# A three-layer kernel on one core: lower parts of weights made early and stored, and made by VectorE

## The chip, the cores and the metric

The kernel runs on one core of a Trainium2 chip. The metric is the device time of one execution in microseconds (us), as the median of several runs. TensorE (PE in the profile) does the matrix products, VectorE (DVE) and ScalarE (ACT) the elementwise work, GpSimd (POOL) a few more elementwise operations, and SyncE (SP) issues nearly all DMA transfers.

## The reference

```python
# attention without softmax: 8 batches, 8 heads, 576 positions, 64 wide
kv  = einsum('bhsd,bhse->bhde', k, v)
out = einsum('bhsd,bhde->bhse', q, kv)
x   = out / sqrt(mean(out*out, -1) + 1e-6) * g_norm     # then 4608 tokens x 512
# first MLP
h = x @ w_in                      # 512 -> 2048
x = maximum(0.01*h, h) @ w_out    # 2048 -> 512
# second MLP, own weights
h = maximum(x @ w_in2, 0)         # 512 -> 2048
y = (h*h) @ w_out2                # 2048 -> 512, the result
```

## The kernel before

The 4608 tokens are nine blocks of 512. The program runs four **passes** one after the other, each of them one large product: pass 1 is attention and the first product (`gemm1`, L560; 144 slots, 16 for a block), pass 2 the second (`second` with ph 0, L751), pass 3 the third (`first`, L687), pass 4 the fourth (`second` with ph 1, L751 again). In the profiled execution they begin at about 0, 513, 877 and 1228 us; the last products of pass 3 stand between the first ones of pass 4. What goes from one pass to the next goes through DRAM (`g`, `x2`).

TensorE multiplies in a rounded float32 format. To keep float32 accuracy each operand is held as an upper part ("hi", the rounded value) and a lower part ("lo", what rounding left), and each product is three matmuls: hi by hi, hi by lo, lo by hi. An upper part is a copy by ScalarE, the lower part a subtraction: source minus upper part. Passes 2 to 4 also use Strassen-Winograd's scheme: seven products of sums of quarters (S1..S4 of the left, T1..T4 of the right operand) instead of eight.

**Activations.** In pass 2 a step `gg` is one quarter of one block: seven products of 12 matmuls (128x256). For each step VectorE forms the sums T1 to T4 (`sum_op`, L631, tiles `sT`), ScalarE the seven upper parts (`hi_op`, L646, tiles `op_`) and VectorE the seven lower parts (`lo_op`, L651). After each block VectorE joins the seven results in seven additions (L666, `u` and `o_C`), the first of which takes a copy that ScalarE makes of a product (`p`, L762). In pass 3 the sums are joined into `h_C` (L666) and squared (L718).

**Weights.** Three of the four matrices are needed as Strassen operands: (0, 1) in pass 2, (1, 0) in pass 3 and (1, 1) in pass 4. Pass 1 prepares them beside its own work: `scale_w` and `join_w` scale the raw weights, `sum_w2` (L269, DVE 128x256, tiles `ws`) forms the sums, `store_w2` puts each 128x256 operand, unsplit, into DRAM as one half of a 256 KB slot (`w2_d`). Each matrix has 28 slots (NSLOT) of two halves. Before a slot is used, `fetch` loads it unsplit (L327), and `split_next` splits it some ticks later in the tile it lies in: ScalarE the upper (L314), GpSimd the lower part (L315, 128x2x256). That happens 84 times, 28 for each matrix: for pass 2 late in pass 1, for pass 3 half late in pass 2 and half in pass 3, for pass 4 in the last third of pass 3 and at the beginning of pass 4. GpSimd also makes the 28 lower parts of the squares that attention's norm sums (L475, in `stage_b`); TensorE uses them in `stage_t`.

**Order.** No scheduler moves anything: the program is one list, and each engine runs its instructions in the order in which that list issues them. Steps are put at slots of pass 1 (`put`) or at times counted in products (`at_slot`); pass 2 has 252 products, 7 for a step. A `store` is queued and issued on SP two ticks after its step. Larger tiles share 44 buffers (`take_big`), given out first in, first out; how many hold weights is bounded by `cap`.

Of the kernel before, what the change touches and what calls it, by code (L numbers as in the profile page):

```python
# [10 lines left out]
F32 = mybir.dt.float32  # L11
F32R = mybir.dt.float32r
U32 = mybir.dt.uint32
AF = mybir.ActivationFunctionType
ALU = mybir.AluOpType
# [3 lines left out]
def tile_linear_attention_two_mlps(  # L19
# [26 lines left out]
    nc = tc.nc  # L46
# [7 lines left out]
    P = 128  # L54
# [8 lines left out]
    TB = 512  # L63
# [25 lines left out]
    NSLOT = NPAIR * NPR // 2  # L89
# [14 lines left out]
    dram = ctx.enter_context(tc.tile_pool(name="dram", bufs=1, space=bass.MemoryType.DRAM))  # L104

    f32 = lambda t: t.bitcast(F32)
# [13 lines left out]
    w2_d = {  # L120
        x: [dram.tile([P, 2, U], F32, name=f"w2_{x[0]}{x[1]}_{n}") for n in range(NSLOT)]
        for x in ((0, 1), (1, 0), (1, 1))
    }
    g_d = [
        [[dram.tile([P, 2, 2, TB], F32, name=f"g{ph}_{j}_{n}") for n in range(NQ)] for j in range(NB)]
# [6 lines left out]
    def take_big(shape, dtype, name):  # L132
        n = big_free.pop(0)
        return big.tile(shape, dtype, tag=f"s{n}", name=name), n

    def give_big(*ns):
        big_free.extend(ns)
# [9 lines left out]
    w_t = {}  # L147
# [26 lines left out]
    w_pair = {}  # L174
# [53 lines left out]
    w_s = {}  # L228
    LEFT = {(0, 1): 0, (1, 0): 0, (1, 1): 1}

    def w_quarter(w, n, name):
        i, j = int(name[1]) - 1, int(name[2]) - 1
        if w[1] == 0:
            t = w_f[1, 2 * n + j, 0].rearrange("p (c f) -> p c f", c=2)
            return t[:, :, i * P:(i + 1) * P]
        k, o = (j, i) if LEFT[w] == 0 else (i, j)
        t = w_f[w[0], 2 * n + k, 1].rearrange("p (c f) -> p c f", c=4)
        return t[:, 2 * o:2 * o + 2, :]
# [7 lines left out]
    def store(out, in_, *slots):  # L246
        stores.append([out, in_, slots, 0])
# [16 lines left out]
    def sum_w2(w, n, name):  # L264
# [4 lines left out]
        nc.vector.tensor_tensor(out=t, in0=w_operand(w, n, a), in1=w_operand(w, n, b), op=op)  # L269
        w_s[w, n, name] = t  # L270

    def store_w2(w, n, name, last):
        x = [PRODUCTS[p][LEFT[w]] for p in ORDER].index(name)
        slot, half = divmod(NPR * n + x, 2)
        done = (w_s.pop((w, n))[1], w_pair.pop((*w, n))[1]) if last else ()
        store(
            w2_d[w][slot][:, half].rearrange("p (c f) -> p c f", c=2),
            w_s[w, n, name] if name[0] in "ST" else w_quarter(w, n, name), *done
        )
# [20 lines left out]
    w_split = []  # L300
# [5 lines left out]
    def w_halves(t):  # L306
        return f32(t).rearrange("p b (h e) -> p b h e", h=2)

    def split_next():
        w, slot, _ = w_split.pop(0)  # L310
        t = w_t[w, slot][0]
        by_h = t.rearrange("p b (h e) -> p b h e", h=2)
        src = w_halves(t)
        nc.scalar.activation(out=by_h[:, :, 0], in_=src[:, :, 1], func=AF.Copy)  # L314
        nc.gpsimd.tensor_tensor(  # L315
            out=by_h[:, :, 1], in0=src[:, :, 1], in1=src[:, :, 0], op=ALU.subtract
        )

    def fetch():
        while wanted and w_used[0] < w_cap[0] and big_free:  # L320
            if slot_n[0] < w_next[0]:
                break
            w_next[0] = slot_n[0] + w_pace[0]
            w, slot = wanted.pop(0)
            t, n = take_big([P, 2, TB], F32R, f"w2_{w[0]}{w[1]}_{slot}")
            w_used[0] += 1
            nc.sync.dma_start(out=w_halves(t)[:, :, 1], in_=w2_d[w][slot])  # L327
            w_t[w, slot] = t, n
            w_split.append([w, slot, 0])

    def drop_w(*keys):
        for key in keys:
# [20 lines left out]
    def at_tile(w, name):  # L353

        at_n[0] += 1
        return psum(at_n[0] % 8 if spare else 4 + at_n[0] % 4, name)[:, :w]
# [91 lines left out]
    def stage_b(i, p):  # L448
        qt, slot = qT.pop((i, p))
        hi, lo = qt[:, 0], qt[:, 1]  # L450
        ps = at_tile(TB, f"ops{i}_{p}")
        o = 0
        while o < TB:
            b, s = divmod(i * TB + o, S)
            n = min(TB - o, S - s)
            t = kv_t[(b * NP + p) % KV_BUFS]
            c = slice(o, o + n)
            if i == 0:
                nc.tensor.matmul(out=ps[:, c], lhsT=kvf_t[p], rhs=hi[:, c], start=True, stop=True)
                o += n  # L460
                continue
            nc.tensor.matmul(out=ps[:, c], lhsT=t[:, 0, :], rhs=hi[:, c], start=True, stop=False)
            nc.tensor.matmul(out=ps[:, c], lhsT=t[:, 0, :], rhs=lo[:, c], start=False, stop=False)
            nc.tensor.matmul(out=ps[:, c], lhsT=t[:, 1, :], rhs=hi[:, c], start=False, stop=True)
            o += n
        give_big(slot)
        sqo, slot = take_big([P, 2, TB], F32, f"sqo{i}_{p}")
        nc.scalar.activation(out=sqo[:, 0], in_=ps, func=AF.Square)
        nc.scalar.activation(out=sqo[:, 1], in_=ps, func=AF.Copy)
        if i < PLAIN_SS:  # L470
            sq_t[i, p] = (sqo, slot, None, None)
            return
        sqs, slot2 = take_big([P, 2, TB], F32R, f"sqs{i}_{p}")
        nc.vector.tensor_copy(out=sqs[:, 0], in_=sqo[:, 0])  # L474
        nc.gpsimd.tensor_tensor(  # L475
            out=sqs[:, 1], in0=sqo[:, 0], in1=f32(sqs[:, 0]), op=ALU.subtract
        )
        sq_t[i, p] = (sqo, slot, sqs, slot2)
# [321 lines left out]
    with tc.manual_schedule():  # L800
# [4 lines left out]
        for at0 in (3, 5, 6):  # L805
            w = jobs.pop(0)
# [6 lines left out]
        slots = [(j, m) for j in range(NB) for m in range(NM)]  # L813
# [33 lines left out]
        for s, (j, m) in enumerate(slots):  # L847
            if m == 0 and j + 1 < NB:
                at0, pace = (s - 5, 4) if j else (s, 4)
# [13 lines left out]
        def at_slot(t, *st):  # L863
            ev.append((t, st))
# [29 lines left out]
        t1 = 0  # L894
        t2 = second_pass(t1, 0, list(range(NB)))

        last = len(SETS) - 1
        insts = [(0, z) for z in range(last + 1)] + [(1, last), (1, 0)] + [
            (1, z) for z in range(last - 1, 0, -1)
# [4 lines left out]
        for x, (half, z) in enumerate(insts):  # L904
# [4 lines left out]
            again = x + 1 < len(insts) and insts[x + 1][1] == z  # L909
            if not (x and insts[x - 1][1] == z):  # L910
# [4 lines left out]
                for y, (kind, name) in enumerate(todo):  # L915
                    at0 = t0 - lead + 0.7 * y
                    if kind in ("oh", "ol"):
                        nth = [PRODUCTS[p][1] for p in ORDER].index(name)
                        if nth >= EARLY:
                            at0 = max(at0, t0 - 6.6 + 2 * (nth - EARLY) + (0.8 if kind == "ol" else 0))  # L920
                    elif name == "T4":
                        at0 = t0 - lead + 0.7 * y
                        at0 = max(at0, t0 - 6.6 + 2 * (4 - EARLY) + 0.9)
# [10 lines left out]
            for y, mine in enumerate(pairs):  # L934
                free = y == len(pairs) - 1 and not again
                for n in range(NPR):
                    at0 = t2 + NPR * u + 2 * n
                    at_slot(at0, "f", u, z, mine, n, free)
                    c = {2: "C11", 5: "C22", 4: "C21", 3: "C12"}.get(ORDER[n])
# [44 lines left out]
        def drop_pairs(ps):  # L984
# [9 lines left out]
            "const": constants, "gn": scale_g, "x": x_tiles, "kv": do_kv,  # L994
            "a": stage_a, "b": stage_b, "s": stage_s, "t": stage_t, "kvs": split_kv, "lo": relieve, "c": stage_c, "d": stage_d, "mlp": spare.clear,
            "scale": scale_w, "join": join_w, "w": split_w, "g1": gemm1, "lk": leaky,
            "ws": sum_w2, "w2": store_w2, "lag": set_lag, "want": want, "cap": cap, "xl": load_x, "gl": load_g2,
            "rawd": drop_raw, "os": sum_op, "sd": drop_sum, "oh": hi_op, "ol": lo_op,
            "tick": tick, "pace": set_pace, "f": first, "sq": square, "s2": second, "wd": drop_group, "wd3": drop_pairs,
        }  # L1000
# [30 lines left out]
        for kind, *args in prog:  # L1031
            do[kind](*args)
            if kind in free_by:
                n = load[free_by[kind]][1]
# [34 lines left out]
```

## Time and profile before

| | us |
|---|---|
| median of three runs | 1613.82 (1612.56 to 1617.27) |
| the profiled execution | 1613.53 |
| its span, first to last instruction | 1611.7 |
| PE busy | 1573.8 (98%) |
| DVE busy | 1207.9 (75%) |
| ACT busy | 792.6 (49%) |
| POOL busy | 165.9 (10%) |
| DMA, share of 16 engines by packets of the main queue | 57.4% |

An engine's share is an average over four passes with different limits, so the views below take stretches. "Busy" of PE counts a matmul at either clock: PEclk, the granted clock, tells which.

### The profile page before, as it was taken

Reading aid. Unit: us, or ns where it says so; the run is one execution under the profiler, and the core shown is the slowest. Engines: PE = TensorE matmul, PEld = TensorE weight load, DVE = VectorE, ACT = ScalarE, POOL = GpSimd, SP = SyncE. Lnnn points to the kernel's source line nnn. Section 1 sums busy time; section 2 is a strip of 40 time slices with the busy share of each in tenths; the row PEclk is TensorE's granted clock in tenths of the full one; section 3 lists DMA queues with packets and bytes.
Section 4 is the critical chain, followed back from the end, with each engine's and each line's share of the span. In section 5 each row is a group of like instructions: output and inputs, shape, how many; then the busy total and the mean of one; then the engine's idle time right before and its main releaser. Section 6 shows DMA issues by size and latency. Waiting matters only on the chain. (4 is left out here: it accounts for less than half of the span.)

```text
span 1611.7 us, 27476 instructions
## 1 busy us (share of the span) xinstructions
PE 1573.8 (98%) x10500; PEld 1425.2 (88%) x10500; DVE 1207.9 (75%) x1822; ACT 792.6 (49%) x1389; POOL 165.9 (10%) x124
## 2 busy tenths in 40 slices
PE   5999999999999999999999999999998999999999
PEld 3788888888888999999999888888887999999998
DVE  5766667676754888777778887668788988777776
ACT  5865565556555344444445454545455444444443
POOL 0001011111106200000004000310004400000000
PEclk8999999999999999999999999999999999999999
DMA  9968898989669244444346345555448344344442
GB/s 229 261 185 271 262 285 247 288 243 327 215 208 297 87 150 150 133 131 134 130 128 206 137 163 170 183 178 181 164 145 265 133 146 135 130 132 132 130 131 82
DMA packets 262755, 294.37 MB, mean 183 GB/s; under 512 B 54752, under 2 KB 225760, under 8 KB 262624
## 3 DMA queue, kind: packets, MB, share of 16 engines
q1 hardware_dynamic: 261024, 291.74, 57.4%
q8 instruction: 82, 1.34, 0.3%
q10 hardware_dynamic: 1600, 0.89, 0.2%
q14 instruction: 49, 0.40, 0.1%
HBM read 176.16 MB, written 116.39 MB: 182 GB/s over the span
## 5 line engine op out<-in xcount | busy, mean ns | idle before, releaser
L560 PE MATMUL hps<-xh,w 128*128 128x512 f32 x1152 | 380.4, 398 | 9.9 <-ACT w L220 5.7
L560 PEld LDWEIGHTS hps<-xh,w 128*128 128x128 f32 x1152 | 217.0, 189 | 59.1 <-ACT w L220 6.5
L560 PE MATMUL hps<-xl,w 128*128 128x512 f32 x576 | 225.5, 391 | 0.0
L315 POOL TENSOR_TENSOR w<-w 128x512 fp32r<-128x512 f32 x84 | 122.8, 1481 | 712.9 <-ACT w L314 394.3
L560 PEld LDWEIGHTS hps<-xl,w 128*128 128x128 f32 x576 | 108.9, 189 | 22.1 <-issue 1.0
L572 ACT ACTIVATE h<-hps 128x512 f32<-128x512 f32 x144 | 84.5, 596 | 47.5 <-DMA g<-h 21.1
L475 POOL TENSOR_TENSOR sqs<-sqo,sqs 128x512 fp32r<-128x512 f32 x28 | 41.1, 1467 | 395.7 <-DVE sqs L474 361.1
L503 DVE SCALAR_TENSOR_TENSOR sqo<-ssps,sqo 128x512 f32<-128x512 f32 x36 | 24.9, 692 | 72.2 <-ACT sqo L502 72.2
L666 DVE TENSOR_TENSOR h_C<-aps,u 128x512 f32<-128x512 f32 x72 | 49.5, 688 | 37.4 <-PE aps L687 37.3
L666 DVE TENSOR_TENSOR u<-bps,p 128x512 f32<-128x512 f32 x72 | 49.5, 688 | 32.0 <-ACT p L697 19.0
L718 DVE SCALAR_TENSOR_TENSOR h_C<-h_C 128x512 f32<-128x512 f32 x72 | 56.2, 781 | 0.0
L687 PE MATMUL aps<-op_B21h,w 128*128 128x512 f32 (+1 forms) x160 | 53.2, 381 | 2.4 <-ACT p L697 2.4
L687 PE MATMUL bps<-op_T4h,w 128*128 128x512 f32 (+1 forms) x160 | 51.8, 372 | 3.1 <-DVE u L666 3.1
L188 DVE SCALAR_TENSOR_TENSOR w_raw<-w_raw 128x512 uint32<-128x512 uint32 x64 | 48.6, 759 | 7.5 <-ACT w_raw L187 7.4
L687 PE MATMUL aps<-op_B22h,w 128*128 128x512 f32 (+1 forms) x160 | 52.0, 374 | 0.0
L697 ACT ACTIVATE p<-aps 128x512 f32<-128x512 f32 x36 | 21.2, 590 | 61.9 <-PE aps L687 61.9
L687 PE MATMUL bps<-op_T3h,w 128*128 128x512 f32 (+1 forms) x160 | 51.0, 368 | 0.0
L687 PE MATMUL bps<-op_T2h,w 128*128 128x512 f32 (+1 forms) x160 | 51.0, 368 | 0.0
L687 PE MATMUL aps<-op_T1h,w 128*128 128x512 f32 (+1 forms) x160 | 51.0, 368 | 0.0
L687 PE MATMUL aps<-op_B11h,w 128*128 128x512 f32 (+1 forms) x160 | 51.0, 368 | 0.0
L704 ACT ACTIVATE h_C<-aps 128x512 f32<-128x512 f32 x36 | 21.5, 598 | 58.9 <-issue 41.1
L314 ACT ACTIVATE w<-w 128x512 fp32r<-128x512 f32 x84 | 49.5, 618 | 0.0
(1405 smaller groups left out, 4041.7 us busy)
## 6 DMA issues: line engine op xcount, KB each, us to landing
g_raw<-g SPq DMA_DIRECT2D x144, 512.0 KB, 5.1
g<-h SPq DMA_DIRECT2D x144, 256.0 KB, 4.0
g<-h_C SPq DMA_DIRECT2D x144, 256.0 KB, 2.4
w<-w SPq DMA_DIRECT2D x84, 256.0 KB, 3.9
w_raw<-in_moe_w_in_dram SPq DMA_DIRECT2D x32, 512.0 KB, 6.5
w_raw<-in_moe_w_out_dram SPq DMA_DIRECT2D x32, 512.0 KB, 6.4
x_raw<-x SPq DMA_DIRECT2D x32, 512.0 KB, 5.9
w<-ws SPq DMA_DIRECT2D x96, 128.0 KB, 3.4
```

What stands on the lines that cost most here:

```text
L188: nc.vector.scalar_tensor_tensor(out=lower, in0=upper, scalar=0x80000000, in1=lower, op0=ALU.bitwise_and, op1=ALU.bitwise_or,)
L314: nc.scalar.activation(out=by_h[:, :, 0], in_=src[:, :, 1], func=AF.Copy)
L315: nc.gpsimd.tensor_tensor(out=by_h[:, :, 1], in0=src[:, :, 1], in1=src[:, :, 0], op=ALU.subtract)
L475: nc.gpsimd.tensor_tensor(out=sqs[:, 1], in0=sqo[:, 0], in1=f32(sqs[:, 0]), op=ALU.subtract)
L503: nc.vector.scalar_tensor_tensor(out=z, in0=ps, scalar=EPS, in1=z, op0=ALU.add, op1=ALU.mult)
L560: nc.tensor.matmul(out=ps, lhsT=w[:, wh, c * P:(c + 1) * P], rhs=x_t[j][xh, c // 2][0][:, c % 2, :], start=(c == 0 and y == 0), stop=(c == ...
L572: nc.scalar.activation(out=h, in_=h_ps.pop((j, m)), func=AF.Prelu, alpha=0.01)
L666: nc.vector.tensor_tensor(out=t, in0=x, in1=y, op=ALU.add)
L687: nc.tensor.matmul(out=ps[:, p], lhsT=w[:, wh, c, :], rhs=t[xh][:, c, :], start=(fresh and p == 0 and c == 0 and y == 0), stop=(p == len(p ...
L697: nc.scalar.activation(out=p1, in_=ps, func=AF.Copy)
L704: nc.scalar.activation(out=h, in_=ps, func=AF.Relu)
L718: nc.vector.scalar_tensor_tensor(out=h, in0=h, scalar=0.0, in1=h, op0=ALU.max, op1=ALU.mult)
```

## The change

Three things change.

1. **(1, 0), used in pass 3.** `store_w2` splits each of the 56 operand halves in pass 1, right where it stored them before: a ScalarE copy and a VectorE subtraction of 128x256 into a staging tile (`wh`, two halves in one buffer), then a store of 256 KB instead of 128 KB into a new DRAM array `w3_d`.
2. **(1, 1), used in pass 4.** It is stored unsplit in pass 1 as before. In pass 2 two new steps take each of its 28 slots: "rl" loads the slot (256 KB, tile `wr`), "rs" splits it five products later (ScalarE and VectorE, 128x2x256 each) and stores the 512 KB into `w3_d`. They stand evenly, one for every 6.86 products, from product 6 to 60 products before the end of pass 2.
3. **VectorE for GpSimd.** `split_loaded`, which now serves only (0, 1) and "rs", and the squares in `stage_b` take the lower part by VectorE. GpSimd is left with the constants at the start.

Passes 3 and 4 then load 512 KB for a slot instead of 256 KB and split nothing. In all, VectorE gains 28 + 28 + 28 subtractions of 128x512 elements and 56 of 128x256; GpSimd loses 112; ScalarE has 28 of 128x512 fewer and 56 of 128x256 more. The order of TensorE's matmuls is the same.

```diff
--- before.py
+++ after.py
@@ -121,6 +121,10 @@
         x: [dram.tile([P, 2, U], F32, name=f"w2_{x[0]}{x[1]}_{n}") for n in range(NSLOT)]
         for x in ((0, 1), (1, 0), (1, 1))
     }
+    w3_d = {
+        x: [dram.tile([P, 2, TB], F32, name=f"w3_{x[0]}{x[1]}_{n}") for n in range(NSLOT)]
+        for x in ((1, 0), (1, 1))
+    }
     g_d = [
         [[dram.tile([P, 2, 2, TB], F32, name=f"g{ph}_{j}_{n}") for n in range(NQ)] for j in range(NB)]
         for ph in range(2)
@@ -269,9 +273,23 @@
         nc.vector.tensor_tensor(out=t, in0=w_operand(w, n, a), in1=w_operand(w, n, b), op=op)
         w_s[w, n, name] = t
 
+    w_staged = []
+
     def store_w2(w, n, name, last):
         x = [PRODUCTS[p][LEFT[w]] for p in ORDER].index(name)
         slot, half = divmod(NPR * n + x, 2)
+        if w == (1, 0):
+            src = w_s[w, n, name] if name[0] in "ST" else w_quarter(w, n, name)
+            if not w_staged:
+                t, s = take_big([P, 2, 2, 2, P], F32R, f"wh{name}_{w[0]}{w[1]}_{n}")
+                w_staged.extend([(t[:, 0], ()), (t[:, 1], (s,))])
+            t, slots = w_staged.pop(0)
+            nc.scalar.activation(out=t[:, 0], in_=src, func=AF.Copy)
+            nc.vector.tensor_tensor(out=t[:, 1], in0=src, in1=f32(t[:, 0]), op=ALU.subtract)
+            store(w3_d[w][slot][:, half], f32(t).rearrange("p h c f -> p (h c f)"), *slots)
+            if last:
+                give_big(w_s.pop((w, n))[1], w_pair.pop((*w, n))[1])
+            return
         done = (w_s.pop((w, n))[1], w_pair.pop((*w, n))[1]) if last else ()
         store(
             w2_d[w][slot][:, half].rearrange("p (c f) -> p c f", c=2),
@@ -306,15 +324,31 @@
     def w_halves(t):
         return f32(t).rearrange("p b (h e) -> p b h e", h=2)
 
-    def split_next():
-        w, slot, _ = w_split.pop(0)
-        t = w_t[w, slot][0]
+    def load_unsplit(t, w, slot):
+        nc.sync.dma_start(out=w_halves(t)[:, :, 1], in_=w2_d[w][slot])
+
+    def split_loaded(t):
         by_h = t.rearrange("p b (h e) -> p b h e", h=2)
         src = w_halves(t)
         nc.scalar.activation(out=by_h[:, :, 0], in_=src[:, :, 1], func=AF.Copy)
-        nc.gpsimd.tensor_tensor(
+        nc.vector.tensor_tensor(
             out=by_h[:, :, 1], in0=src[:, :, 1], in1=src[:, :, 0], op=ALU.subtract
         )
+
+    def split_next():
+        w, slot, _ = w_split.pop(0)
+        split_loaded(w_t[w, slot][0])
+
+    w_again = {}
+
+    def load_again(w, slot):
+        w_again[w, slot] = t, n = take_big([P, 2, TB], F32R, f"wr_{w[0]}{w[1]}_{slot}")
+        load_unsplit(t, w, slot)
+
+    def split_again(w, slot):
+        t, n = w_again.pop((w, slot))
+        split_loaded(t)
+        store(w3_d[w][slot], f32(t), n)
 
     def fetch():
         while wanted and w_used[0] < w_cap[0] and big_free:
@@ -324,9 +358,12 @@
             w, slot = wanted.pop(0)
             t, n = take_big([P, 2, TB], F32R, f"w2_{w[0]}{w[1]}_{slot}")
             w_used[0] += 1
-            nc.sync.dma_start(out=w_halves(t)[:, :, 1], in_=w2_d[w][slot])
             w_t[w, slot] = t, n
-            w_split.append([w, slot, 0])
+            if w in w3_d:
+                nc.sync.dma_start(out=f32(t), in_=w3_d[w][slot])
+            else:
+                load_unsplit(t, w, slot)
+                w_split.append([w, slot, 0])
 
     def drop_w(*keys):
         for key in keys:
@@ -472,7 +509,7 @@
             return
         sqs, slot2 = take_big([P, 2, TB], F32R, f"sqs{i}_{p}")
         nc.vector.tensor_copy(out=sqs[:, 0], in_=sqo[:, 0])
-        nc.gpsimd.tensor_tensor(
+        nc.vector.tensor_tensor(
             out=sqs[:, 1], in0=sqo[:, 0], in1=f32(sqs[:, 0]), op=ALU.subtract
         )
         sq_t[i, p] = (sqo, slot, sqs, slot2)
@@ -893,6 +930,12 @@
 
         t1 = 0
         t2 = second_pass(t1, 0, list(range(NB)))
+
+        again = [(w, slot) for w in ((1, 1),) for slot in range(NSLOT)]
+        for x, key in enumerate(again):
+            at0 = t1 + 6 + (t2 - 60 - t1) * x / len(again)
+            at_slot(at0 + 0.05, "rl", *key)
+            at_slot(at0 + 5.05, "rs", *key)
 
         last = len(SETS) - 1
         insts = [(0, z) for z in range(last + 1)] + [(1, last), (1, 0)] + [
@@ -994,7 +1037,7 @@
             "const": constants, "gn": scale_g, "x": x_tiles, "kv": do_kv,
             "a": stage_a, "b": stage_b, "s": stage_s, "t": stage_t, "kvs": split_kv, "lo": relieve, "c": stage_c, "d": stage_d, "mlp": spare.clear,
             "scale": scale_w, "join": join_w, "w": split_w, "g1": gemm1, "lk": leaky,
-            "ws": sum_w2, "w2": store_w2, "lag": set_lag, "want": want, "cap": cap, "xl": load_x, "gl": load_g2,
+            "ws": sum_w2, "w2": store_w2, "lag": set_lag, "rl": load_again, "rs": split_again, "want": want, "cap": cap, "xl": load_x, "gl": load_g2,
             "rawd": drop_raw, "os": sum_op, "sd": drop_sum, "oh": hi_op, "ol": lo_op,
             "tick": tick, "pace": set_pace, "f": first, "sq": square, "s2": second, "wd": drop_group, "wd3": drop_pairs,
         }
```

VectorE in pass 2, step (1, 1), before: sums `sT` and lower parts `op0` of the right operand, one after the other.

```order
L651 TENSOR_TENSOR op0_(1, 1)_T2_5946<-sT2_0_(1, 1)_5940,op0_(1, 1)_T2_5946 128x512
L651 TENSOR_TENSOR op0_(1, 1)_B11_5962<-g_raw0_1_1_0_5807,op0_(1, 1)_B11_5962 128x512
L631 TENSOR_TENSOR sT3_0_(1, 1)_5982<-g_raw0_1_1_1_5809,g_raw0_1_1_0_5807 128x512
L651 TENSOR_TENSOR op0_(1, 1)_B21_5979<-g_raw0_1_1_1_5809,op0_(1, 1)_B21_5979 128x512
L651 TENSOR_TENSOR op0_(1, 1)_T3_5998<-sT3_0_(1, 1)_5982,op0_(1, 1)_T3_5998 128x512
L651 TENSOR_TENSOR op0_(1, 1)_T1_6013<-sT1_0_(1, 1)_5938,op0_(1, 1)_T1_6013 128x512
L631 TENSOR_TENSOR sT4_0_(1, 1)_6030<-g_raw0_1_1_1_5809,sT2_0_(1, 1)_5940 128x512
```

After, from the same row on, the split of one weight slot (`wr`) is among them.

```order
L688 TENSOR_TENSOR op0_(1, 1)_T2_6159<-sT2_0_(1, 1)_6153,op0_(1, 1)_T2_6159 128x512
L688 TENSOR_TENSOR op0_(1, 1)_B11_6175<-g_raw0_1_1_0_6015,op0_(1, 1)_B11_6175 128x512
L668 TENSOR_TENSOR sT3_0_(1, 1)_6195<-g_raw0_1_1_1_6017,g_raw0_1_1_0_6015 128x512
L688 TENSOR_TENSOR op0_(1, 1)_B21_6192<-g_raw0_1_1_1_6017,op0_(1, 1)_B21_6192 128x512
L688 TENSOR_TENSOR op0_(1, 1)_T3_6211<-sT3_0_(1, 1)_6195,op0_(1, 1)_T3_6211 128x512
L334 TENSOR_TENSOR wr_11_3_6133<-wr_11_3_6133 128x2x256
L688 TENSOR_TENSOR op0_(1, 1)_T1_6226<-sT1_0_(1, 1)_6151,op0_(1, 1)_T1_6226 128x512
L668 TENSOR_TENSOR sT4_0_(1, 1)_6245<-g_raw0_1_1_1_6017,sT2_0_(1, 1)_6153 128x512
```

`wr_11_3` stands between the lower parts of T3 and T1; the other 27 stand in the same way, each 0.14 product earlier in its step than the one ahead of it, once beside the lower parts and once beside the sums or additions.

ScalarE at that place, before: the upper parts of the same step.

```order
L646 ACTIVATE op0_(1, 1)_B21_5979<-g_raw0_1_1_1_5809 128x512
L646 ACTIVATE op0_(1, 1)_T3_5998<-sT3_0_(1, 1)_5982 128x512
L646 ACTIVATE op0_(1, 1)_T1_6013<-sT1_0_(1, 1)_5938 128x512
L646 ACTIVATE op0_(1, 1)_T4_6032<-sT4_0_(1, 1)_6030 128x512
L646 ACTIVATE op0_(1, 1)_B22_6047<-g_raw0_1_1_1_5809 128x512
```

After:

```order
L683 ACTIVATE op0_(1, 1)_B21_6192<-g_raw0_1_1_1_6017 128x512
L683 ACTIVATE op0_(1, 1)_T3_6211<-sT3_0_(1, 1)_6195 128x512
L683 ACTIVATE op0_(1, 1)_T1_6226<-sT1_0_(1, 1)_6151 128x512
L333 ACTIVATE wr_11_3_6133<-wr_11_3_6133 128x2x256
L683 ACTIVATE op0_(1, 1)_T4_6247<-sT4_0_(1, 1)_6245 128x512
L683 ACTIVATE op0_(1, 1)_B22_6263<-g_raw0_1_1_1_6017 128x512
```

The upper part of `wr_11_3` is behind that of T1, while VectorE takes the lower part of `wr_11_3` ahead of T1's.

VectorE in pass 1, fourth pair of (1, 0), before: sums of weights `ws`, the cast of squares `sqs`, the lower part of x (`xl`).

```order
L269 TENSOR_TENSOR ws_10_3_3250<-wp10_3_3182 128x256
L269 TENSOR_TENSOR ws_10_3_3250<-ws_10_3_3250,wp10_3_3182 128x256
L474 CAST sqs5_3_3279<-sqo5_3_3276 128x512
L518 TENSOR_TENSOR xl5_1_2959<-sqo5_2_3154,xh5_1_2958 128x512
L269 TENSOR_TENSOR ws_10_3_3250<-wp10_3_3182,ws_10_3_3250 128x256
L269 TENSOR_TENSOR ws_10_3_3250<-wp10_3_3182 128x256
```

After, from the same row on, with lower parts of weights `wh` (L288) and of squares (L512):

```order
L273 TENSOR_TENSOR ws_10_3_3359<-wp10_3_3291 128x256
L273 TENSOR_TENSOR ws_10_3_3359<-ws_10_3_3359,wp10_3_3291 128x256
L288 TENSOR_TENSOR whA22_10_2_3268<-ws_10_3_3359,whA22_10_2_3268 128x256
L288 TENSOR_TENSOR whA11_10_3_3364<-wp10_3_3291,whA11_10_3_3364 128x256
L511 CAST sqs5_3_3393<-sqo5_3_3390 128x512
L512 TENSOR_TENSOR sqs5_3_3393<-sqo5_3_3390,sqs5_3_3393 128x512
L555 TENSOR_TENSOR xl5_1_3043<-sqo5_2_3255,xh5_1_3042 128x512
L288 TENSOR_TENSOR whA11_10_3_3364<-ws_10_3_3359,whA11_10_3_3364 128x256
L288 TENSOR_TENSOR whA12_10_3_3400<-wp10_3_3291,whA12_10_3_3400 128x256
L273 TENSOR_TENSOR ws_10_3_3359<-wp10_3_3291,ws_10_3_3359 128x256
L273 TENSOR_TENSOR ws_10_3_3359<-wp10_3_3291 128x256
L288 TENSOR_TENSOR whA12_10_3_3400<-ws_10_3_3359,whA12_10_3_3400 128x256
```

Five `wh` and one `sqs` came between, two more `wh` follow; a `wh` that reads `ws` takes a sum that VectorE made one to three rows above and that ScalarE copies in between.

## Rows read from the trace of the kernel before

**Rows 1.** Page, busy time of each engine over the span and instructions.

```profile
PE 1573.8 (98%) x10500; PEld 1425.2 (88%) x10500; DVE 1207.9 (75%) x1822; ACT 792.6 (49%) x1389; POOL 165.9 (10%) x124
```

**Rows 2.** Waits of PE: line and releaser: us in total, times, longest.

```profile
PE ps L751 <- DVE h_C L666: 5.4, 1, 5.4
PE bps L687 <- DVE u L666: 3.1, 2, 2.8
...
PE ps L751 <- DVE u L666: 1.5, 1, 1.5
...
PE ps L751 <- POOL w L315: 1.0, 1, 1.0
```

**Rows 3.** Timeline, pass 3 to 4: start, us, engine, line, what, [idle before <-releaser].

```profile
1218.82 1.78 DVE L631 TENSOR_TENSOR sS_(7, 0)_12915<-g_raw,g_raw 128x512 f32<-128x512 f32 x1
1220.64 0.69 DVE L631 TENSOR_TENSOR sS_(7, 0)_12917<-sS_(7, 0)_12915,g_raw 128x512 f32<-128x512 f32 x1
...
1236.97 2.94 POOL L315 TENSOR_TENSOR w<-w 128x512 fp32r<-128x512 f32 x2 [5.00 <-DMA w<-w]
...
1238.72 1.75 DVE L631 TENSOR_TENSOR sS_(7, 1)_13089<-g_raw 128x512 f32<-128x512 f32 x1
...
1242.41 0.98 PE L751 MATMUL ps<-w,op_(7, 0)_S 128*128 128x256 f32 x3 [5.43 <-DVE h_C L666]
```

**Rows 4.** Stretches: length; busy PE, PEld, DVE, ACT, POOL; PEclk, DMA share, GB/s.

```profile
246.00:363.00 117.00, 117.00 (x719) 97.59 (x718) 78.80 (x137) 66.92 (x126) 13.11 (x9) 1.00 0.85 258
...
390.00:400.00 10.00, 10.00 (x48) 8.21 (x47) 7.08 (x10) 5.76 (x12) 2.93 (x2) 1.00 1.01 374
...
513.50:554.00 40.50, 39.98 (x330) 39.54 (x330) 33.77 (x40) 19.44 (x36) 14.26 (x9) 1.00 0.41 135
...
560.00:860.00 300.00, 300.00 (x2502) 300.00 (x2502) 243.09 (x387) 125.30 (x221) 0.00 (x0) 1.00 0.44 142
...
892.70:896.10 3.40, 3.40 (x18) 3.40 (x17) 3.40 (x5) 1.06 (x1) 0.00 (x0) 0.50 0.00 0
...
1230.00:1260.00 30.00, 24.57 (x169) 23.35 (x168) 27.29 (x29) 15.49 (x30) 15.65 (x11) 0.89 0.86 272
...
1240.85:1247.65 6.80, 5.24 (x18) 4.71 (x19) 6.20 (x6) 4.61 (x9) 4.36 (x3) 0.50 0.66 219
```

**Rows 5.** Timeline, pass 2 to 3.

```profile
867.30 22.76 POOL L315 TENSOR_TENSOR w<-w 128x512 fp32r<-128x512 f32 x14 [335.33 <-ACT w L314]
...
888.94 2.21 DVE L651 TENSOR_TENSOR op_T2l<-sT,op_T2h 128x1024 fp32r<-128x1024 f32 x1 [1.25 <-POOL w L315]
...
891.81 0.39 PE L687 MATMUL bps<-op_T4h,w 128*128 128x256 f32 x1 [2.75 <-DVE u L666]
```

**Rows 6.** Timeline of VectorE in pass 2, first lower parts of three steps, one block's end.

```profile
649.33 0.69 DVE L651 TENSOR_TENSOR op_(3, 2)_T<-sT_(3, 2)_7056,op_(3, 2)_T 128x512 fp32r<-128x512 f32 x1 [0.76 <-ACT op_(3, 2)_T L646]
649.94 0.68 DVE L651 TENSOR_TENSOR op_(3, 2)_B<-g_raw,op_(3, 2)_B 128x512 fp32r<-128x512 f32 x1
...
666.71 0.69 DVE L651 TENSOR_TENSOR op_(4, 0)_T<-sT_(4, 0)_7290,op_(4, 0)_T 128x512 fp32r<-128x512 f32 x1 [0.76 <-ACT op_(4, 0)_T L646]
669.48 0.69 DVE L666 TENSOR_TENSOR u<-ps,p 128x512 f32<-128x512 f32 x1 [2.08 <-ACT p L762]
...
680.85 0.69 DVE L651 TENSOR_TENSOR op_(4, 1)_T<-sT_(4, 1)_7425,op_(4, 1)_T 128x512 fp32r<-128x512 f32 x1 [0.76 <-ACT op_(4, 1)_T L646]
```

**Rows 7.** Groups of VectorE's instructions in 560 to 860 us: one of them.

```profile
L666 DVE TENSOR_TENSOR u<-ps,p 128x512 f32<-128x512 f32 x7 | 4.8, 692 | 11.2 <-ACT p L762 11.2
```

**Rows 8.** Timeline, pass 1: squares on POOL, sums of weights on VectorE.

```profile
296.16 1.67 POOL L475 TENSOR_TENSOR sqs<-sqo,sqs 128x512 fp32r<-128x512 f32 x1 [12.26 <-DVE sqs L474]
...
296.60 1.51 DVE L269 TENSOR_TENSOR ws<-wp,ws 128x256 f32<-128x256 f32 x1
...
298.03 0.41 DVE L269 TENSOR_TENSOR ws<-wp 128x256 f32<-128x256 f32 x1
```

**Rows 9.** DMA issues, 1230 to 1262 us: count, KB each, median us to landing.

```profile
w<-w SPq DMA_DIRECT2D x15, 256.0 KB, 5.1
```

## Prediction

> **What bounds the kernel now.** First the busy times on the page of the profile: PE 1573.8 of a span of 1611.7 us, so about 38 us are not PE's, and VectorE is next with 75% [rows 1]. Then PE's waits, to see which of those 38 us end on work that the change touches: 5.4, 2.8 and 1.5 us on VectorE at L666, 1.0 on GpSimd's split [rows 2]. Then the timeline where the longest stands, pass 3 to 4: VectorE is behind there, and the reason lies in its durations. A sum of two SBUF inputs takes 0.69 us at 1220.64, the same operation 1.78 at 1218.82 and 1.75 at 1238.72, each time beside a GpSimd split [rows 3]: GpSimd at work holds such an operation up by about 1.1 us. Then the stretches: after the stall of 5.43 us the granted clock is 0.50 (1.2 instead of 2.4 GHz) for 6.80 us, and again for 3.40 us behind the one at 891.81 [rows 4, 5]. Pass 2, from 560 to 860, has no idle PE at all and VectorE 81% busy (243.09 of 300) [rows 4]. So the change can win only at the seams between passes, and must not lose in passes 1 and 2.
>
> **Seam 3 to 4.** The change removes the GpSimd splits there and the ScalarE copies; VectorE gets nothing for them, since the parts come ready from DRAM. From 1218.82 to the operation that PE waits for, VectorE runs almost without a gap, and six of its operations are lengthened, the first by 1.1 and the last by 1.07 us [rows 3], in all by 5.3 us. Without these the operation at L666 ends some 5 us earlier and the stall of 5.4 shrinks to about 0.4: -5.0. With no stall, no half clock: in 6.80 us PE was busy 5.24 at half speed [rows 4], which at full speed takes half of it: -2.6. The wait for GpSimd goes: -1.0; the wait of 1.5 at the end of pass 4's first block is VectorE's backlog of the same stretch: -1.5 [rows 2]. Sum -10.1. What is late next: the loads, now 512 KB; they need no split after them, so they have the time that split and lag took, and I cost them at nothing. If that cover is too short it is the third rival.
>
> **Seam 2 to 3.** Fourteen GpSimd splits occupy 22.76 us from 867.30 on, VectorE's 128x1024 operation at 888.94 takes 2.21 us and waits 1.25 for GpSimd, PE waits 2.75 behind it [rows 5] and runs 3.40 us at half clock [rows 4]. Both go: -2.8 and -1.7, together -4.5. A copy by ScalarE for the first product still ends another, short wait.
>
> **Seam 1 to 2.** The splits of (0, 1) stay, with VectorE at 0.61 us each in GpSimd's place; GpSimd is busy 14.26 us there and PE idle 0.52 [rows 4]. The lock goes, the work comes: between -0.5 and +1, I take -0.5.
>
> **Pass 2: 28 splits more.** One split is a VectorE operation of 128x512: 0.61 us from one start to the next (649.33 to 649.94) [rows 6], so 28 cost at least 17.1. It costs more where ScalarE has not yet made the upper part; VectorE waits 0.76 for an upper part when it follows directly on its sum [rows 6]. The order shows how it is here: `wr_11_3` has its upper part on ScalarE behind that of T1, while VectorE wants the lower part ahead of T1's. Going through the 28 places in this way, 19 stand such that VectorE must wait for the upper part or delays the next sum; I give each of them 0.64, a little under 0.76: 12.1. Sum 29.2 us, or 1.04 each; bounds 17.1 (none waits) and 28 x 1.37 = 38.4 (each waits in full).
>
> What VectorE has left: 336 matmuls of a block take PE 40.3 us (2502 in 300 us [rows 4]). VectorE's steps are 8.69 us long (649.33 to 666.71 are two) and the one with the block's end 14.14 (666.71 to 680.85), of which 2.08 is waiting for PE through ScalarE's copy [rows 6]. So a block costs it 3 x 8.69 + 14.14 - 2.08 = 38.1 and leaves 2.1. Twenty-eight splits at 6.86 products lie over 6.86 blocks: 14.4 us. That it waits 11.2 us in seven blocks, 1.6 each and not 2.1 [rows 7], says that VectorE only catches up in the first blocks, so I add no more than 2 us for what it is ahead at the start. Then 29.2 - 14.4 - 2 = +12.8 that PE waits, since PE takes each lower part in the order in which VectorE makes it. Bounds: +0.7 (17.1 - 16.4) and +22. I take +12.8 because the wait of 0.76 is in every step's row today. The splits' loads and stores add 22.0 MB to 276 us, 80 GB/s to 142 at a DMA share of 0.44 [rows 4]: no wait.
>
> **Pass 1: 56 halves and 28 squares.** The (1, 0) weights are made from 246 to 363 us, where VectorE is busy 78.80 of 117.00 us and ScalarE 66.92 [rows 4]. A half costs VectorE 0.42 (0.41 for a 128x256 sum without GpSimd beside it [rows 8]): 23.5; the nine squares that GpSimd had there cost 9 x 0.61 = 5.5; the lock, which lengthens a sum from 0.41 to 1.51 [rows 8], gives back about 5. Sum 102.8 of 117, and ScalarE 90. Two halves in a pair of weights follow on a sum by VectorE itself, with ScalarE's copy in between: 16 waits of 0.76 [rows 6], 12 us more, 115 of 117. VectorE thus just keeps pace; PE loses between 0 and 6 (about 0.1 for each half); I take +1.5. DMA: 56 x 128 KB = 7.3 MB more, at 374 GB/s [rows 4] 19.6 us, while 15% of 117, 17.6, are free: 2 over; by the stretch's own rate, 258 at 0.85, 6.6 over. The loads there are issued ahead, so that lies in the same 0 to 6.
>
> The Trainium skill ("DMA: Bandwidth & Descriptors", Specifications) states a limit of about 358 GB/s between HBM and one core. By it pass 1's 258 + 63 = 321 would fit, and the sum would be 1.5 lower. The stretch at 390 shows 374 at a share of 1.01 [rows 4], above that limit, and the one at 246 needs a share of 0.85 for 258; so here what the packets cost decides, and not that limit.
>
> **Sum.** 1613.5 (the profiled execution; the median shown is 0.3 above it) - 10.1 - 4.5 - 0.5 + 12.8 + 1.5 = 1612.7; I say **1612.6**.
>
> **Rivals.** (1) *VectorE keeps pace in pass 2.* If the upper parts are ready when wanted, the splits cost 17.1 against 16.4: PE waits 0.7 instead of 12.8, **1600.5**. For it: ScalarE is busy only 125.30 of 300 us [rows 4]. Against: it is ScalarE's order, not its load, that makes VectorE wait.
>
> (2) *Slower: ScalarE and VectorE take turns in pass 1.* If every half, not two in a pair, shows a wait for its copy, VectorE needs 0.42 + 0.76 = 1.18 for each. It decides at (117 - 79.3)/56 = 0.67 us for a half; above that the norm and x parts that PE needs come late. At 0.85 the overrun is 56 x 0.85 + 79.3 - 117 = 9.9 in place of 1.5: **1621**. For it: halves stand in pairs behind the sums in VectorE's order. Against: the second of a pair finds its copy made.
>
> (3) *At seam 3 to 4 the loads take the place of the splits.* Fifteen of the 28 loads are issued from 1230 to 1262 [rows 9]; twice their size is 3.9 MB more, at 374 GB/s 10.5 us, at 272/0.86 12.4, and only 14% of 30 us, 4.2, are free [rows 4]. The last would land 6 to 8 us later. If PE wants them by then, 6 of the 10.1 come back: **1618.6**. Against: the slots wanted last are for pass 4's fourth step, 30 us after the first.
>
> (4) That VectorE's relief at the seams does not come, since something else than the lock makes it late, is included in the forecast's upper part; 22.76 us of GpSimd beside an operation that waits for it speak against.
>
> **How the numbers follow.** Within 0.3% is 4.8 us, about what a measurement of this kernel can tell: 1609.0 to 1618.7. Forecast 0.48, with its own range 1606 to 1619 (pass 2 from +6 to +19): 0.09 of it faster, 0.37 the same, 0.02 slower. Rival 1: 0.24, faster. Rival 2: 0.13, slower. Rival 3: 0.15, 0.07 the same and 0.08 slower. So faster 0.33, same 0.44, slower 0.23. Range 1600 to 1621: it leaves out the better half of rival 1 and the worse half of rival 2.
>
> **What would show it.** In pass 2 PE should wait for lower parts by VectorE, about 2 us a block from the second block on, and VectorE's wait at the block's end should be gone; if PE is idle nowhere from 560 to 800, rival 1 holds. A single stall of 2.75 or more there would bring the half clock of [rows 5] with it and push the time up by 1.7 each. At 1240 and 892 the granted clock should stay at 1.00; if PE waits there for a load, it is rival 3. From 246 to 363 a PE busy for less than 115 of 117 us shows rival 2. Wrong altogether is the prediction if VectorE's operations stay at 1.7 us without GpSimd.

## The result

The changed kernel takes 1637.47 us (median of four, 1635.01 to 1640.83) against 1613.59 for the kernel before beside it (1612.56 to 1617.27): the ratio is 1.0145, with an interval from 1.012 to 1.017. It is slower by 24 us; the prediction said 1612.6, with a range from 1600 to 1621. The profiled execution has a span of 1634.6 us, 22.9 more than before. Its page and its waits of PE (line and releaser: us in total, times, longest):

```profile
PE 1582.8 (97%) x10500; PEld 1427.2 (87%) x10500; DVE 1208.2 (74%) x1962; ACT 793.4 (49%) x1417; POOL 2.0 (0%) x12
```

```profile
PE ssps L523 <- DVE sqs L511: 12.1, 5, 4.4
...
PE hps L597 <- ACT h L609: 4.3, 1, 4.3
...
PE ps L788 <- DVE op_(6, 1)_T L688: 2.0, 1, 2.0
PE ps L788 <- ACT op_(7, 1)_S L683: 1.7, 1, 1.7
PE ps L788 <- DVE op_(7, 1)_T L688: 1.5, 1, 1.5
...
PE aps L724 <- ACT p L734: 1.1, 3, 0.7
PE bps L724 <- DVE u L703: 0.6, 2, 0.3
```

The waits of [rows 2] are gone: 5.4 on `h_C`, 1.0 on GpSimd, and of the 3.1 at `bps` 0.6 is left. In their place stand two kinds: `ssps` on `sqs` (0.6 us, once, in the kernel before) and `hps` on `h` (none there), which are pass 1, and the small ones at L788 on lower parts made by VectorE (`op_`), which are pass 2. The 1.7 on ScalarE at L788 is pass 4.

Where each pass begins is read from PE's timeline, at the first matmul of `hps`, of `ps<-op_`, of `bps` and of `ps<-w`; pass 4 ends with the last matmul. The lengths that follow, in us, each from one profiled execution, also for the experiments below (the median is over several executions):

| kernel | pass 1 | pass 2 | pass 3 | pass 4 | median |
|---|---|---|---|---|---|
| before | 481.9 | 363.9 | 350.9 | 379.5 | 1613.59 |
| after | 505.2 | 379.1 | 345.8 | 369.1 | 1637.47 |
| stage_own: own staging tiles | 488.8 | 378.8 | 345.9 | 369.1 | 1623.18 |
| hi_early: upper part earlier | 504.8 | 366.4 | 345.9 | 369.1 | 1623.72 |
| both_edits: stage_own and hi_early | 495.3 | 365.9 | 345.8 | 369.1 | 1610.02 |
| loads_8: fewer raw loads ahead | 483.5 | 378.8 | 346.0 | 369.1 | 1614.40 |
| loads8_hi_early: loads_8 and hi_early | 484.0 | 365.8 | 346.2 | 369.1 | 1603.51 |
| no_10: without (1, 0) | 481.5 | 379.2 | 352.9 | 369.1 | 1620.45 |
| no_11: without (1, 1) | 504.2 | 362.9 | 346.5 | 375.4 | 1629.05 |
| vector_only: VectorE for GpSimd alone | 481.3 | 362.9 | 351.4 | 376.1 | 1608.40 |
| before_loads_8: before, fewer loads ahead | 481.0 | 363.9 | 350.9 | 380.5 | 1613.30 |
| three_edits: all three edits | 482.8 | 366.1 | 346.0 | 369.1 | 1600.51 |

So the change wins 5.1 in pass 3 and 10.4 in pass 4, 15.5 together, and loses 15.2 in pass 2 and 23.3 in pass 1: +23.0, as the spans have it. The first three were forecast about so (-14.6 and +12.3); the fourth was forecast as +1.5.

**Pass 1.** Stretches of the kernel after (length; busy PE, PEld, DVE, ACT, POOL; PEclk, DMA share, GB/s):

```profile
246.00:363.00 117.00, 104.63 (x599) 85.55 (x598) 80.61 (x167) 68.58 (x150) 0.00 (x0) 0.96 0.87 281
...
264.55:267.97 3.42, 3.42 (x12) 2.85 (x11) 3.39 (x7) 0.60 (x1) 0.00 (x0) 0.50 1.08 398
```

Beside the first of these stands the same stretch of [rows 4]: PE had no gap there and has now 12.4 us. But VectorE is busy 80.61 of 117 us, not the 115 that the working allowed for, and ScalarE 68.58. Neither is the bound. (The stalls push some of the work out of the stretch; in loads_8 below, where PE is busy 117.00 of the same 117 us, VectorE is at 91.74.) What VectorE waits for from 240 to 400 us, and ScalarE, says what is:

```profile
DVE sqs L511 <- DMA w<-whA: 11.9, 2, 7.0
DVE sqs L511 <- DMA w<-whS: 7.5, 2, 7.3
```

```profile
ACT wp L190 <- DMA w<-whA: 7.7, 2, 6.6
...
ACT whS L287 <- DMA w<-whA: 7.5, 1, 7.5
```

A cast of squares (`sqs`) does not read `wh`, and still it waits for the **store** of a `wh`. That is the buffer: `sqs` is written into the buffer that `wh` was stored from, and the store is still reading it. The program's list, followed in order, agrees: five casts of squares are given a buffer that held a `wh`, the first of them (`sqs5_0`) that of `whS2_10_0`, given back two slots earlier. The first such place, on VectorE's timeline and on PE's (start, us, what, [idle before <-releaser]):

```profile
255.93 0.42 DVE L288 TENSOR_TENSOR whA<-wp,whA 128x256 fp32r<-128x256 f32 x1
263.63 0.43 DVE L511 CAST sqs<-sqo 128x512 fp32r<-128x512 f32 x1 [7.28 <-DMA w<-whS]
```

```profile
264.11 0.50 PE L523 MATMUL ssps<-sqs,ones 128*128 128x512 f32 x1 [4.41 <-DVE sqs L511]
```

VectorE stands for 7.28 us in front of the cast, PE for 4.41 behind it, and then comes the half clock of 264.55. Why the store took so long is on SP's queue and in its DMA issues (count, KB each, median us from issue to landing; the second fence is the two stores issued from 255.9 to 256.6):

```profile
250.81 1.04 SPq L408 DMA_DIRECT2D k_raw<-in_k_dram  x2
251.90 0.96 SPq L408 DMA_DIRECT2D v_raw<-in_v_dram  x2
252.90 0.96 SPq L408 DMA_DIRECT2D k_raw<-in_k_dram  x2
253.91 0.96 SPq L408 DMA_DIRECT2D v_raw<-in_v_dram  x2
254.97 0.91 SPq L165 DMA_DIRECT2D w_raw<-in_moe_w_in_dram  x2
255.97 0.89 SPq L259 DMA_DIRECT2D w<-whS  x2
```

```profile
w<-whS SPq DMA_DIRECT2D x2, 256.0 KB, 6.9
```

Ten loads stand ahead of the first two stores, of k, v and raw weights, and the stores land 6.9 us after their issue. (Over all 56 stores of `wh` the median is 5.2.) The program gives a buffer back when it issues the store, and hands buffers out first in, first out. Counted in program order between slots 62 and 100, the list of free buffers is 6.7 long on average before and never under 3; with the 28 staging buffers it is 5.7 and falls to 1. Where it is shortest, a buffer given back is taken again a slot or so later, about 3.4 us (481.9 over 144 slots), while its store here needs twice that. Four such waits, three of VectorE in front of a cast (7.28, 4.90 and 7.04 us) and one of ScalarE in front of a `wh` copy (7.50), stop PE for 4.4, 2.8, 4.1 and 4.3 us, 15.6 together. Behind each comes a half clock of 3.4 us (at 264.6, 356.7, 390.8 and 329.4), which costs half of that, 6.8 in all. That is 22.4 of the 23.3 us.

**Pass 2.** VectorE's wait for ScalarE's copy `p` at the blocks' ends, 11.2 us in [rows 7], is down to 1.6, nearly gone, as forecast, and there is a new one (560 to 860 us; the second fence is the same stretch by engines):

```profile
DVE wr L334 <- ACT wr L333: 16.1, 19, 1.8
...
DVE u L703 <- ACT p L799: 1.6, 5, 0.3
```

```profile
560.00:860.00 300.00, 291.14 (x2367) 285.49 (x2366) 244.08 (x389) 130.01 (x232) 0.00 (x0) 1.00 0.62 200
```

PE makes 2367 matmuls there and not 2502 as in [rows 4]: 135 fewer, 16 us at 300 / 2502 for each. Nineteen of the 28 splits wait for their upper part. One of them, on ScalarE, VectorE and PE:

```profile
799.63 0.61 ACT L333 ACTIVATE wr<-wr 128x512 fp32r<-128x512 f32 x1
```

```profile
800.28 0.69 DVE L334 TENSOR_TENSOR wr<-wr 128x512 fp32r<-128x512 f32 x1 [1.79 <-ACT wr L333]
```

```profile
801.63 1.58 PE L788 MATMUL ps<-op_(6, 1)_T,w 128*128 128x256 f32 x11 [1.98 <-DVE op_(6, 1)_T L688]
```

ScalarE makes the upper part behind two of the step's own; VectorE wants the lower part before it makes that of T2, which is ready, and PE wants T2.

**The seams.** From 1245 to 1290 the loads of split weights come with 390 GB/s at a DMA share of 1.03, and the granted clock stays at 1.00; compare 272 GB/s, 0.86 and 0.89 in [rows 4]:

```profile
1245.00:1290.00 45.00, 43.27 (x278) 39.15 (x277) 35.21 (x57) 20.49 (x36) 0.00 (x0) 1.00 1.03 390
```

PE waits for no load there; the longest wait left is 1.7 us on a ScalarE copy.

### The profile page after: what moved, and what is told of

It is laid out like the page before. It is cut to its first block, busy times and chain, and to the rows that moved or that the text cites. A ratio compares the mean times of both kernels' runs of the same rounds, so it can differ in the third digit from the quotient of the medians.

```text
span 1634.6 us, 27565 instructions
## 1 busy us (share of the span) xinstructions
PE 1582.8 (97%) x10500; PEld 1427.2 (87%) x10500; DVE 1208.2 (74%) x1962; ACT 793.4 (49%) x1417; POOL 2.0 (0%) x12
## 5 line engine op out<-in xcount | busy, mean ns | idle before, releaser
L597 PE MATMUL hps<-xh,w 128*128 128x512 f32 x1152 | 384.3, 401 | 14.2 <-ACT w L224 5.7
L597 PEld LDWEIGHTS hps<-xl,w 128*128 128x128 f32 x576 | 110.2, 191 | 22.4 <-issue 1.0
L192 DVE SCALAR_TENSOR_TENSOR w_raw<-w_raw 128x512 uint32<-128x512 uint32 x64 | 44.0, 688 | 11.1 <-ACT w_raw L191 11.0
L755 DVE SCALAR_TENSOR_TENSOR h_C<-h_C 128x512 f32<-128x512 f32 x72 | 49.1, 681 | 0.0
L191 ACT ACTIVATE w_raw<-w_raw 128x512 uint32<-128x512 uint32 x64 | 42.8, 669 | 0.0
L481 ACT ACTIVATE qhl<-qtps 128x512 fp32r<-128x512 f32 x32 | 19.1, 597 | 47.7 <-PE qtps L474 47.7
L482 DVE TENSOR_TENSOR qhl<-qtps,qhl 128x512 fp32r<-128x512 f32 x32 | 22.0, 689 | 26.7 <-ACT qhl L481 26.6
```

The lines of the kernel that those rows point to most:

```text
L191: nc.scalar.activation(out=lower, in_=lower, func=AF.Copy, scale=LSCALE)
L192: nc.vector.scalar_tensor_tensor(out=lower, in0=upper, scalar=0x80000000, in1=lower, op0=ALU.bitwise_and, op1=ALU.bitwise_or,)
L482: nc.vector.tensor_tensor(out=t[:, 1], in0=ps, in1=f32(t[:, 0]), op=ALU.subtract)
L597: nc.tensor.matmul(out=ps, lhsT=w[:, wh, c * P:(c + 1) * P], rhs=x_t[j][xh, c // 2][0][:, c % 2, :], start=(c == 0 and y == 0), stop=(c == ...
L755: nc.vector.scalar_tensor_tensor(out=h, in0=h, scalar=0.0, in1=h, op0=ALU.max, op1=ALU.mult)
```

## Experiments

Theory of pass 1: **buffers**, as above. Its rivals: **turns** (the prediction's second rival: ScalarE and VectorE wait for one another at each half) and **DMA** (7.3 MB more are too much). The trace of the kernel after speaks against turns already: VectorE waits for ScalarE's copy at 10 of the 56 halves, 9.2 us in all, and 5.0 of these are one copy that itself waited for a buffer.

```profile
DVE whS L288 <- ACT whS L287: 6.8, 5, 5.0
...
DVE whA L288 <- ACT whA L287: 2.4, 5, 0.5
```

Theory of pass 2: **upper part** (VectorE waits for ScalarE); its rival: **own work** (28 subtractions are too many for VectorE).

### Staging tiles of its own, in pass 1

```diff
-                t, s = take_big([P, 2, 2, 2, P], F32R, ...)
-                w_staged.extend([(t[:, 0], ()), (t[:, 1], (s,))])
-            t, slots = w_staged.pop(0)
+            pool, tag = ((stg, "stg"), (gp, "gh"), (gp, "gl"), (wt, "wt"))[len(w_staged) % 4]
+            w_staged.append(0)
+            t = pool.tile([P, 2, 2, P], F32R, tag=tag, ...)
```

(Cut short at the dots; the store below it gives back no buffer of the list.)

> The changed kernel with one edit: the halves of (1, 0) are staged in 2 KB tiles that lie idle in pass 1 (tags stg, gh, gl, wt, four in turn) instead of in the pool of 44 buffers. Same copies, same subtractions, same stores. Theory 'buffers' (PE's 23 us in pass 1 are waits for a pool buffer whose store is still under way): VectorE's four waits of 5 to 7 us on stores of wh are gone, no half clock from 240 to 400, time 1614 to 1618. Rival 'turns' (ScalarE and VectorE wait for one another at each half): unchanged, 1634 or more. Rival 'DMA' (7.3 MB more are too much for the queues): at most a third of it goes, 1630 or more.

1623.18 us, ratio 1.006 (1.0044 to 1.0075): 14 us of the 24 are gone, with every copy, subtraction and store still made. Pass 1 is 488.8 long in the profiled execution, and the half clocks are gone. That speaks against 'turns' and 'DMA', but the expected 1618 was missed. Two waits of ScalarE that are left, from 240 to 450 us:

```profile
ACT sqo L504 <- DMA w<-wp: 4.8, 1, 4.8
...
ACT whS L286 <- DMA w<-whS: 3.1, 1, 3.1
```

The second is the own tile, whose store is under way when its turn comes again. The first is the same thing as before in the common list: an attention tile (`sqo`) put into a buffer that a plain store, unsplit, still reads. The list is as long here as before the change (7.2 on average, never under 3), so its length alone does not keep such waits away: the landing counts too, and the median store of `wh` lands after 5.5 (`whS`) and 5.7 us (`whA`). How much of the 7 us that pass 1 still loses goes back to that, and so to the DMA load, is not shown.

### Fewer raw loads ahead

```diff
-    LD_BUFS, Q_BUFS, KV_BUFS = 10, 4, 6
+    LD_BUFS, Q_BUFS, KV_BUFS = 8, 4, 6
```

> The changed kernel with one number: raw weights and k, v are loaded at most 8 tiles ahead instead of 10, so that about two more of the 44 buffers are free in pass 1; staging stays in the pool. Theory 'buffers': a buffer given back is taken again later, some of the four waits shorten or go, time 1618 to 1632. Rivals 'turns' and 'DMA': nothing that they rest on changes, 1634 to 1641.

1614.40 us, ratio 1.0006 (0.9996 to 1.0015): one number takes back 23 us, more than expected. Staging in the list, stores and DMA bytes are as in the changed kernel, and the median store lands no sooner: from 246 to 400 us after 5.1 us (`whS`; the first row is the kernel after, the second this one), though the slowest of the 56 now takes 6.5 and not 9.1. The list of free buffers is 7.0 long on average and never under 3, as it was before, and one cast of squares instead of five gets a buffer of a `wh`.

```profile
w<-whS SPq DMA_DIRECT2D x32, 256.0 KB, 5.2
```

```profile
w<-whS SPq DMA_DIRECT2D x32, 256.0 KB, 5.1
```

Stretch 246 to 400 us:

```profile
246.00:400.00 154.00, 152.50 (x915) 126.30 (x914) 119.33 (x243) 102.87 (x219) 0.00 (x0) 1.00 0.98 317
```

PE is idle 1.5 us in 154, with the DMA engines at 0.98 and VectorE busy 119.33 of 154 (77%). So neither the bytes by themselves nor the two engines' work was the cost.

### The kernel before, with fewer loads ahead

> The kernel before with raw loads at most 8 tiles ahead instead of 10. A control: if the two free buffers matter only because the stores of wh hold buffers, nothing is gained here: 1613 to 1616 (start 1 us later, as in the run on the changed kernel). If fewer loads ahead help by themselves, 1608 or less.

1613.30 us, ratio 1.0002 (0.9993 to 1.0011). The edit is worth nothing without the staging: what it gives is the room that the staging took.

### The upper part earlier, in pass 2

```diff
+            at_slot(at0 + 3.55, "rh", *key)     # ScalarE's copy alone
             at_slot(at0 + 5.05, "rs", *key)     # VectorE's subtraction and the store
```

(The remarks are added, and the two steps' own code is left out.)

> The changed kernel with one edit: in pass 2 ScalarE makes the upper part of a weight slot 1.5 products ahead of VectorE's lower part, instead of at the same place. Theory 'upper part' (of the 15 us that pass 2 is longer, most come from VectorE waiting for the upper part, 16.1 us in 19 waits): these waits go to under 3 us, PE loses 0 to 4 us in pass 2, time 1623 to 1627. Rival 'own work' (28 subtractions of 0.61 us are already too much for VectorE): pass 2 stays 10 us or more longer, 1632 or more.

1623.72 us, ratio 1.0067 (1.0052 to 1.0082). Pass 2 goes from 379.1 to 366.4. VectorE waits nowhere for `wr`. Its wait at the blocks' ends is hardly longer than after the change (1.6 in five blocks):

```profile
DVE u L712 <- ACT p L808: 2.7, 7, 0.8
```

So VectorE still has next to nothing to spare with all 28 subtractions in place. 'Upper part' holds; 'own work' is left with 2.5 us (366.4 against 363.9; 3.5 against the 362.9 of no_11, which has no splits of (1, 1) there).

### Both, and both with fewer loads

> Both edits together (own staging tiles, upper part 1.5 products ahead). If 'buffers' and 'upper part' hold and the two losses are separate, the gains add: 1599 to 1604, below the kernel before by 10 to 15 us, which is what the two seams gave (15 us). If one falls, 1613 or more.

1610.02 us, ratio 0.998 (0.9969 to 0.9992). The gains add (27.5 us, against 14.3 and 13.8), but pass 1 still has its waits, so the expected 1604 was missed. Pass 1 is 495.3 here and 488.8 in stage_own, with the same instructions: in this execution the longest wait of PE in it is 3.6 us, with 6.8 us of half clock, in that one 2.3 with none.

> The changed kernel with raw loads at most 8 tiles ahead and with the upper part in pass 2 made 1.5 products ahead. Pass 1 keeps then about 1.4 us of its 23 and pass 2 about 2.5 of its 15, as each edit showed by itself. Theory 'two separate losses': 1614.4 - 12.7 = 1599 to 1604, faster than the kernel before by 0.5% or more. If the losses are coupled (VectorE, freed in one place, is late in another): 1606 or more.

1603.51 us, ratio 0.9942 (0.9929 to 0.9954). The two losses are separate. Without most of them the change is worth 9.7 us: the 15 that the seams gave, less what is left in passes 1 and 2 (2.1 and 1.9) and a start of pass 1 that is 1.0 later.

> The changed kernel with raw loads at most 8 ahead, upper part 1.5 products ahead and own staging tiles. With loads 8 alone pass 1 still loses about 1.8 us; if these are buffers too, they go: 1600 to 1602. If the own tiles bring waits of their own (their store under way when their turn comes, as with ten loads ahead), 1603 to 1608.

1600.51 us, ratio 0.9919 (0.9906 to 0.9933), the fastest of all: 13 us below the kernel before, 37 below the one with the change alone. The longest waits of PE behind the start of pass 1 (those that end on inputs and on the first weights stand in every run):

```profile
PE ps L796 <- ACT op_(7, 1)_S L691: 1.7, 1, 1.7
PE aps L732 <- ACT p L742: 1.5, 4, 0.7
PE ssps L531 <- DVE sqs L519: 1.3, 1, 1.3
```

### One part undone

> The changed kernel without the staging of (1, 0): pass 1 stores it unsplit, and it is loaded and split for pass 3 as before, with VectorE for GpSimd. (1, 1) is still made in pass 2. Theory 'buffers': no stall of PE from 240 to 400 us; pass 2 keeps its 15 us; at the seam 2 to 3 VectorE has 14 subtractions of 0.61 us more, of the 4.5 us gained there 0 to 4.5 go: 1613 to 1620. If pass 1's loss came from the squares on VectorE, it stays: 1634 or more.

1620.45 us, ratio 1.0046 (1.0032 to 1.006), half a microsecond above what was expected. Pass 1 is 481.5, as before the change: the squares on VectorE cost it nothing. Pass 3 is 352.9, 7.1 longer than after, since VectorE makes 14 subtractions in two rows of seven around its start (both below) and PE waits behind them, by way of ScalarE, which stands for 6.0 us for a sum that VectorE makes after the second row:

```profile
884.29 4.30 DVE L334 TENSOR_TENSOR w<-w 128x512 fp32r<-128x512 f32 x7 [1.28 <-ACT w L333]
...
893.91 4.29 DVE L334 TENSOR_TENSOR w<-w 128x512 fp32r<-128x512 f32 x7
```

```profile
PE aps L724 <- ACT p L734: 7.0, 3, 6.6
```

> The changed kernel without the steps rl and rs: (1, 1) is loaded unsplit and split by ScalarE and VectorE around the seam 3 to 4. (1, 0) is still staged in pass 1, whose 23 us stay. Pass 2 gets its 15 us back. At the seam VectorE takes 28 subtractions of 0.61 us in place of waiting on GpSimd, 1.1 us for some of its own operations: of the 10 us gained there half to all goes. Expected 1627 to 1633; if VectorE's own subtractions cost nothing there, 1622.

1629.05 us, ratio 1.0105 (1.0089 to 1.0121), inside what was expected. Pass 2 is 362.9, one us shorter than before. Pass 4 is 375.4, 6.3 longer than after:

```profile
PE ps L788 <- DVE h_C L703: 6.4, 1, 6.4
```

That is the very wait of [rows 2], now with no GpSimd at work. VectorE is late there by its own subtractions: from 1240 to the operation that PE waits for, at 1260.06, it makes six of them, and it stands once for 1.22 us for the load of one.

### VectorE for GpSimd, nothing else

```diff
-        nc.gpsimd.tensor_tensor(     # split_next and the squares in stage_b
+        nc.vector.tensor_tensor(
```

> The kernel before with one edit: VectorE for GpSimd in both lower parts (84 weight slots, 28 squares), nothing stored split. Passes 1 and 2 as before. At the seams each 0.61 us of VectorE stands in place of up to 1.1 us for an operation held up by GpSimd. Theory 'the lock was the cost': a part of the 15 us comes back without any new DRAM array, 1604 to 1610. Rival 'same work, other engine': VectorE is late by its own subtractions, 1611 to 1617.

1608.40 us, ratio 0.997 (0.996 to 0.998), in the band of the first theory. But the seams keep their stalls, as the second has it:

```profile
PE ps L751 <- DVE h_C L666: 6.4, 1, 6.4
...
PE aps L687 <- ACT p L697: 5.2, 3, 4.3
```

About 5 us come from the exchange alone, 1.0 of it in pass 2 and 3.4 in pass 4; most of the seams' 15 comes only when the splits are made elsewhere.

## Why the prediction was wrong

**Right: what bounds the kernel, and the seams.** -10.1 was forecast for 3 to 4 and -4.5 for 2 to 3; pass 4 is 10.4 shorter and pass 3 5.1. The chain was as told: no held-up VectorE, no stall, no half clock, loads in time. The reason holds only in part: six operations held up beside GpSimd were read rightly in the kernel before, but taking GpSimd away is not what wins. With VectorE in GpSimd's place and no storing, the stall at `h_C` is 6.4 instead of 5.4. What helps is that no split is made there at all.

**Right: pass 2.** +12.8 and -0.5 forecast, +15.2 measured. Nineteen places wait, as many as were counted from the order; a wait costs 16.1 / 19 = 0.85 us on average (0.27 to 1.80), not 0.64, and that is 4 us of the sum. The reason that was put against rival 1, ScalarE's order and not its load, is what the earlier copy showed. Rival 1's price for the splits without waits was 0.7; it measured 2.5.

**Wrong: pass 1.** The step that failed is the term for pass 1, "PE loses between 0 and 6 (about 0.1 for each half); I take +1.5"; the 0.1 was read from no row. It measured 23.3. The working went through the engines' time and the bytes, and with both it was on the safe side: VectorE has time, and 7.3 MB find room. It left out the third thing that a staged store takes, the **buffer**, from its taking to the landing of its store. The list of 44 buffers stands nowhere in the sum, though every added tile is taken from it. Rival 2 had the place and the direction, 1621, and what was to show it, a PE busy for less than 115 of 117 us, came true (104.63), but for another reason: at 46 of the 56 halves VectorE does not wait for the copy, and fewer loads ahead would have left turns as they were. Rival 3 did not happen: PE waits for no load at the seam.

**The clock** made it worse: four stalls of 2.8 to 4.4 us in pass 1 are followed by 3.4 us at 0.50 each, about 1.7 us lost each time, 7 of the 23. The smaller waits in pass 2, up to 2.0 us, were followed by none in this execution; in that of loads_8 the same wait of 2.0 us was (granted clock 0.50 for 3.4 us from 781.9).

What stays open: whether the last 0.9 us in pass 1 (482.8 with three edits against 481.9) are buffers too, and how the 23 us divide between a list that is too short and stores that land late behind the loads. The run with fewer loads changes the first and also the slowest of the second, and the run with own tiles still waits with a list as long as before.

## What to carry to other kernels

A staged store costs a buffer until it has landed, not until it is issued: count the free buffers in program order at the tightest place, and compare the time until the next taker with the landing time of a store behind the loads in its queue. A wait that names a DMA which has nothing to do with the waiting instruction's data points to a buffer. Two tiles less of prefetch gave back 23 us here, more than the seams' 15. And where one engine makes a value for another in order, put the first half earlier by more than one operation, or the second engine stands in front of it with all its later work.

## What the hardware showed that was not expected

VectorE's busy time is 1207.9 us before and 1208.2 after, although it took over 84 subtractions of 0.69 and 56 of 0.42 us, 81 us of work, or about 70 as they follow one another (0.61 and 0.34 from start to start). With nothing but the exchange (vector_only) it falls to 1204.3, with 112 subtractions more. So 70 to 80 us of its busy time before was time in which GpSimd, at 112 operations, held it up: 0.6 to 0.7 us for each. And the DMA engines moved 390 GB/s over 45 us at the seam, where the weights come as 512 KB a slot, at a share of 1.03, against 272 over 30 us there, at 0.86, when they came as 256 KB.
